# Cosine attention and a highway layer on one core: separate PSUM tiles for the gate and highway halves of the late output tiles, another split of work between engines, and another planned order

## The chip, the cores and the metric

The kernel runs on one core of a Trainium2 chip. The metric is the device time of one execution in microseconds (us). Most numbers here are medians of several executions; a profile is one execution, taken apart by the hardware profiler. An execution counts as slow when it is over 1.5% above the fastest of the same kernel, else as fast. Ratios use fast executions alone; a median is of all of them, and where some were slow the text says so.

In the profile's lines PE is TensorE, PEld its weight loads, DVE VectorE, ACT ScalarE, POOL GpSimd and SP SyncE. A row of a timeline gives start and duration in us, engine, line of the kernel, operation, the tile written and the tiles read, shapes and count; in brackets the idle time before it and what ended that.

## The reference

```python
# q, k, v: (8, 12, 448, 64) float32, tau = 0.1; w_h, w_t: (768, 768); b_t: (768,)
q_n = q / (norm(q) + 1e-6);  k_n = k / (norm(k) + 1e-6)
attn = softmax(q_n @ k_n.T / tau) @ v            # per batch and head
x = attn.transpose(0, 2, 1, 3).reshape(3584, 768)
H = relu(x @ w_h)
T = sigmoid(x @ w_t + b_t)
out = T * H + (1 - T) * x
```

## The kernel before

The work is cut in 24 head groups of four heads (an index Q) and 28 output tiles of 128 tokens (an index n), each of which is done in two halves of 384 columns. A head group's q and k are squared, summed and normalized, turned (transposed, by TensorE, or by a DMA transpose), multiplied to scores in PSUM (tile `sp`), put through exp (ACT), and multiplied with v (tile `u`); VectorE divides and writes x. An output tile turns x, multiplies it with the gate's weights and the highway's weights, and joins the two. T is computed with tanh, so that each half takes, on VectorE, a bias step (unless the bias is added by one more matmul), and two or three steps to join gate, highway and x.

The kernel doesn't issue instructions in the order of its loops. Each piece of work is recorded as an operation with an engine, a planned duration, its dependencies and a due time; then a planner on the host picks, for each engine, what comes next. Its choice weighs start against due time:

```python
    LAT = {"PE": 260, "ACT": 170, "DVE": 150, "POOL": 150, "SP": 0}
    LATE = 0.025
...
                    k = (max(s, t + self.NEAR) + (e != "SP") * self.LATE * 1000 * o.pri, o.pri, o.n)
...
            if o.size:                                   # a transfer: its share of the DMA engines
                dma_free = max(dma_free, end + 900) + o.size
                o.done = dma_free + 1100
```

Tables of letters say which engine does a piece, one letter per head group or output tile (D DVE, A ACT, P POOL; for XT, S is a DMA transpose; for GATE, R is the three-step form and D and P compute a gate product on that engine; for BIAS, M adds the bias by matmul; for VM, U casts a group's v in two halves on DVE):

```python
    XT = "DDDDDDSDSAASSSSSSDSSSSSSDAAA"
    GATE = "RRRRRRRRRRRRRRRRRRRRPPPPRRRR"
    BIAS = "MMMMMMMMMMMMMMMMMMMMMMDDDDDD"
    VM = "AAAAAAUDUDDDDDDDUDDDAAAA"
    TAIL = 6
```

The last six output tiles (`tail`) come after all scores, so they may use the score tiles. Gate (w_i = 1) and highway (w_i = 0) of a half share one tile of two banks:

```python
            tail = n >= 28 - TAIL
            if not tail:
                ringq, waitq = P.buf("pt", 2)
            elif w_i == 1:
                ringq, waitq = P.buf("sp", 2)
...
                    if tail and w_i == 1 and grp[0] == 0:
                        loc["sp", mh] = s_ps.tile([128, 2, 512], FP32, name="sp")
                    if grp[0] == 0:
                        loc["pt", qi] = (
                            loc["sp", mh][:, 1 - w_i, 0:MH] if tail
                            else p_ps.tile([128, MH], FP32, name="pt", tag="pt")[:, :]
                        )
```

Of the kernel before, what the change touches and what calls it, by code (L numbers as in the profile page):

```python
# [8 lines left out]
FP32 = mybir.dt.float32  # L9
# [11 lines left out]
class Plan:  # L21
# [6 lines left out]
    SLACK = 1.3  # L28
    AHEAD = 15
    NEAR = 60  # L30
    LATE = 0.025

    def __init__(self):
        self.ops = []
# [20 lines left out]
    def run(self):  # L55
        for o in self.ops:
            deps, after = {}, {}
            for d in o.deps:
                if isinstance(d, Op):
                    deps[d.n] = d  # L60
                elif d[0] == "all":
                    deps.update((x.n, x) for x in d[1] if x is not o)
                else:
                    after.update((x.n, x) for x in d[1][:1] if x is not o)
            o.after = [x for n, x in after.items() if n not in deps]
            o.deps = list(deps.values())
        t_eng = {e: 0 for e in self.LAT}
        left = {o.n: len(o.deps) + len(o.after) for o in self.ops}
        outs = {o.n: [] for o in self.ops}
        for o in self.ops:  # L70
            for d in o.deps + o.after:
                outs[d.n].append(o)
        ready = {e: [] for e in self.LAT}
        users = {n: len(c) for n, c in outs.items()}
        back = [o for o in self.ops if not users[o.n]]
        while back:
            o = back.pop()
            due = 1e9 if o.pri is None else o.pri[0] if isinstance(o.pri, tuple) else o.pri
            for c in outs[o.n] if not isinstance(o.pri, tuple) else ():
                lat = o.dur + self.LAT[o.eng] + (o.size + 2000 if o.size else 0)  # L80
                due = min(due, c.pri - (self.SLACK * lat / 1000 if o in c.deps else 0))
            o.pri = due
            for d in o.deps + o.after:
                users[d.n] -= 1
                if not users[d.n]:
                    back.append(d)

        def arm(o):
            r = 0
            for d in o.deps:  # L90
                r = max(r, d.done + (100 if d.eng == o.eng else self.LAT[d.eng]))
            for d in o.after:
                r = max(r, d.start)
            if o.eng == "SP":
                r += 300
            if o.kind == "load":
                r = max(r, 1000 * (o.pri - self.AHEAD))
            if o.kind == "at":
                r = max(r, 1000 * o.pri)
            ready[o.eng].append((r, o))  # L100

        for o in self.ops:
            if not left[o.n]:
                arm(o)
        order = []
        mode = ""
        port = [0, 0]
        dma_free = 0
        lanes = []
        while len(order) < len(self.ops):  # L110
            best = None
            for e, L in ready.items():
                if not L:
                    continue
                t = t_eng[e]
                pick = None
                for r, o in L:
                    s = max(t, r)
                    if e == "DVE" and o.kind == "lock":
                        s = max(s, port[0])  # L120
                    elif e == "POOL":
                        s = max(s, port[1])
                    elif e == "SP" and len(lanes) >= 8:
                        s = max(s, lanes[-8])
                    if e == "SP":
                        s = max(s, dma_free - 5000)
                    k = (max(s, t + self.NEAR) + (e != "SP") * self.LATE * 1000 * o.pri, o.pri, o.n)
                    if pick is None or k < pick[0]:
                        pick = (k, s, r, o)
                if best is None or pick[1] < best[1]:  # L130
                    best = pick
            _, s, r, o = best
            e = o.eng
            ready[e].remove((r, o))
            end = s + o.dur
            if e == "PE":
                if o.kind != mode:
                    end += self.SWITCH
                mode = o.kind
            elif e == "POOL":  # L140
                port[0] = end
            elif e == "DVE" and o.kind == "lock":
                port[1] = end
            t_eng[e] = end
            o.start, o.done = s, end
            if o.size:
                dma_free = max(dma_free, end + 900) + o.size
                o.done = dma_free + 1100
            if e == "SP":
                lanes.append(o.done)  # L150
            order.append(o)
            for c in outs[o.n]:
                left[c.n] -= 1
                if not left[c.n]:
                    arm(c)
        return order
# [6 lines left out]
def kernel(  # L163
# [13 lines left out]
    B, NH, S, D = q.shape  # L177
# [40 lines left out]
    ones_row = const.tile([128, 128], FP16)  # L218
    eps = const.tile([128, 1], FP32)
    NV = 2  # L220
    SQ_E = ("DPAAAAAAPAAAAAPAADPAAAAP", "PPAPPPPPPAAPAAAAAAPPPPPP")
    FOLDS = "000000000002012110000110"
    NORM = ("DDDPPDPPPPPPPPPPPPPPDPPP", "DPPPPPPPPPPPPPPPPPPPPDPP")
    TURN = ("ADDDSSSSSSSSSSSSSSSSSSSS", "DDDDASSSSSSSSSSSSSSSSSSS")
    XT = "DDDDDDSDSAASSSSSSDSSSSSSDAAA"
    ENG = {"A": "ACT", "D": "DVE", "P": "POOL"}
    PAIR = 12
    GATE = "RRRRRRRRRRRRRRRRRRRRPPPPRRRR"
    BIAS = "MMMMMMMMMMMMMMMMMMMMMMDDDDDD"
    LATER = 3  # L230
    W_AT = 16
    RS = "AAAAAAADDDDDDDDDDDDDDDDD"
    SW_AT = 48
    VM = "AAAAAAUDUDDDDDDDUDDDAAAA"
    TAIL = 6
    vm_b = [const.tile([128, 6, C, 66], FP16, name=f"vm{i}") for i in range(NV)]
    e_b = [const.tile([128, 14 * S + 64], FP16, name=f"e{i}") for i in range(2)]
# [40 lines left out]
    def load_qk(Q):  # L278
# [4 lines left out]
        for t in range(2):  # L283
            def f(t=t):
                if t == 0:
                    st["raw", Q] = raw_p.tile([128, NG, D], FP32, name="raw")
                eng = nc.scalar if Q == 0 and t else nc.sync
                eng.dma_start(
                    st["raw", Q][:, NT * t : NT * t + NT].rearrange("x (h c) d -> x h (c d)", h=2),
                    (q, k)[t][b, 4 * qd : 4 * qd + 4]  # L290
                    .rearrange("n (p c) d -> (n p) (c d)", c=C)
                    .rearrange("(h x) f -> x h f", x=128),
                )
            o = op("SP", 60 if Q == 0 and t else 550, None, wait, f, kind="load", size=1300)
            wait = [("first", [o])] + wait if not got else wait
            got.append(o)
            ring.append(o)
        st["got", Q] = got

    def load_v(b):  # L300
# [4 lines left out]
        for i in range(NQ):  # L305
# [7 lines left out]
                    .rearrange("(i x) f -> x i f", x=128),  # L313
                )

            o = op("SP", 550, None, [("first", ring[:1])] + wait if i else wait, f, kind="load", size=1300)
            ring.append(o)
            st["gotv", b].append(o)

# [191 lines left out]
    def norms(Q, rs_op):  # L511
        b, qd = divmod(Q, NQ)
        for t in range(2):
# [50 lines left out]
            else:  # L564
# [4 lines left out]
                        st["qn", Q, t][:, :, :].rearrange("p c x -> p (c x)"),  # L569
                    )  # L570

                z = op("SP", 1230, None, done + wait2, g, size=1330)
                ring += [z]
            ring2.append(z)
            st["turned", Q, t] = z
# [180 lines left out]
    def ffn(b, t, F, n):  # L756
# [25 lines left out]
            nc.sync.dma_start_transpose(loc["xT"][:, :, :], xf())  # L782

        if XT[n] == "S":
            c = a = op("SP", 1100, None, need + waitt, td, size=1140)
        else:
            ringp, waitp = P.buf("pt", 2)
            a = op("PE", 300, None, need + waitp, tr, kind="full")
# [6 lines left out]
    def quarters(b, t, F, n, loc, c, ringt, ring_x, xf, later):  # L795
        ringo, waito = P.buf("o", N_O)
        fin = []
        for qi, (w_i, mh) in enumerate(((1, 0), (0, 0), (1, 1), (0, 1))):
# [1 line left out]
            if qi == LATER:  # L800
                later()
            tail = n >= 28 - TAIL
            if not tail:
                ringq, waitq = P.buf("pt", 2)
            elif w_i == 1:
                ringq, waitq = P.buf("sp", 2)
            when = F + 1.6 * qi
            by_mm = BIAS[n] == "M"
            groups = ((0, 1, 2), (3, 4, 5, 6)) if w_i == 1 and by_mm else ((0, 1, 2), (3, 4, 5))
            mms = []  # L810
            for gi, grp in enumerate(groups):
                def mm(grp=grp, w_i=w_i, ms=ms, mh=mh, qi=qi, tail=tail, by_mm=by_mm):
                    if tail and w_i == 1 and grp[0] == 0:
                        loc["sp", mh] = s_ps.tile([128, 2, 512], FP32, name="sp")
                    if grp[0] == 0:
                        loc["pt", qi] = (
                            loc["sp", mh][:, 1 - w_i, 0:MH] if tail
                            else p_ps.tile([128, MH], FP32, name="pt", tag="pt")[:, :]
                        )
                    for cc in grp:  # L820
# [5 lines left out]
                        )  # L826
                m = op("PE", 163 * len(grp), when + 0.5 * gi,
                       [c, w_done[w_i][gi]] + w_done[2:] * (len(grp) == 4)
                       + ([("first", mms[:1])] if mms else [("first", mms_t[:1])] if tail and w_i == 0 else waitq),
                       mm, kind="full")  # L830
                mms.append(m)
            ringq += mms
            ringt += mms

            if w_i == 1:
                mms_t = mms
                ready = mms[-1]
                if not by_mm:
                    def fb(qi=qi, ms=ms):
# [119 lines left out]
    for Q in range(NQUAD):  # L959
# [6 lines left out]
        elif qd == NQ - 1:  # L966
            o = rsqrt(b, 0, NQ, reds[Q - 2] + reds[Q - 1] + reds[Q])
            for i in range(NQ):
                rs_of[Q - i] = o

    for Q in range(NQUAD):
        norms(Q, rs_of[Q])
    for b in range(B):
        cast_v(b)
        for qd in range(NQ):
            quad(NQ * b + qd)
    todo = []
    for b in range(B):
        f0 = slot_t[NQ * (b + 1)] + 5
        for t in [0, 1, 2] + ([3] if b % 2 else []):  # L980
            todo.append((b, t, f0 + 6.3 * t, len(todo)))
    nxt = [ffn(*todo[0])]

    def more(i):
        if i < len(todo):
            nxt.append(ffn(*todo[i]))

    for i in range(len(todo)):
        nxt[i](lambda i=i: more(i + 1))

    for o in P.run():
        o.fn()
# [35 lines left out]
```

## Time and profile before

| | before |
|---|---|
| time, median of 3 runs | 288.83 us (287.86 to 289.18) |
| span in the profile | 286.2 us |
| last exp ends | 239.8 us |
| last matmul ends | 279.6 us |
| last VectorE step ends | 282.0 us |
| the output lands | 4.2 us later |

The page's first part gives busy time, share of the span and instruction count of each engine:

```profile
PE 241.4 (84%) x4223; PEld 135.9 (47%) x4223; DVE 225.7 (79%) x481; ACT 206.5 (72%) x283; POOL 155.6 (54%) x166
```

No engine stands above 84%, because this is an average over stages that have different limits. One term is needed for the rest of this document: **the tail** is the time from the end of the last exp to the end of the last VectorE step. It is 42.1 us here.

### The profile page before, as it was taken

What the parts mean: (1) busy time and instruction counts of PE and PEld (TensorE: products, weight loads), DVE (VectorE), ACT (ScalarE), POOL (GpSimd) and SP (SyncE); (2) the same over time, 40 slices, a digit from 0 to 9 for tenths busy, and PEclk for the clock granted to TensorE, in tenths of its full rate; (3) what the DMA queues carried; (4) which work ended last, traced back from release to release, by engine and by line L of the source; (5) the groups of instructions that cost most, each with busy time, mean ns of one, the idle gap of its engine ahead of it and who ended that gap; (6) DMA issues with size and microseconds to landing.
All of it is one profiled execution on the core that took longest, in us unless ns stands there. A gap on an engine that the chain in (4) does not pass through costs nothing.

```text
span 286.2 us, 9911 instructions
## 1 busy us (share of the span) xinstructions
PE 241.4 (84%) x4223; PEld 135.9 (47%) x4223; DVE 225.7 (79%) x481; ACT 206.5 (72%) x283; POOL 155.6 (54%) x166
## 2 busy tenths in 40 slices
PE   0278869998998999989989999989999998877660
PEld 0235544554455456454555555555555545544330
DVE  3878876799999979898999999999557454666662
ACT  1599999998985899976987978767897775112210
POOL 3878878536549964993595859708500253620000
PEclk9999999999999999999999999999999999999996
DMA  7999979999999999999999999967954342111112
GB/s 260 382 383 293 210 179 272 243 372 227 351 259 196 250 319 280 217 304 257 264 194 276 247 326 250 240 115 117 170 127 120 85 66 76 55 57 55 57 55 55
DMA packets 72860, 59.14 MB, mean 207 GB/s; under 512 B 49136, under 2 KB 69104, under 8 KB 72816
## 3 DMA queue, kind: packets, MB, share of 16 engines
q1 hardware_dynamic: 70944, 55.69, 76.3%
q0 software_dynamic: 1600, 2.36, 4.6%
q8 instruction: 33, 0.54, 0.8%
q10 hardware_dynamic: 272, 0.46, 0.4%
q14 instruction: 11, 0.09, 0.2%
HBM read 38.14 MB, written 11.01 MB: 172 GB/s over the span
## 4 chain that ended last, share of the span: by engine, by line
PE 38%; DVE 31%; ACT 13%; POOL 7%; issue 5%; DMA 3%; ACTq 0%; DVEq 0%; POOLq 0%
PE pt L821 17%; ACT e L634 8%; PE u L674 8%; PE sp L623 7%; PE sp L821 5%; DVE o L915 4%; DVE n L391 4%; DVE pt L893 3%; DVE pt L908 3%; POOL qn L527 3%; DVE x L725 3%; ACT tt L850 2%; DVE sp L840 2%; DVE vm L586 2%; DVE qn L527 2%
## 5 line engine op out<-in xcount | busy, mean ns | idle before, releaser
L634 ACT ACTIVATE e<-sp 128x896 f16<-128x896 f32 x168 | 145.8, 928 | 25.2 <-PE sp L623 24.4
L527 POOL TENSOR_TENSOR qn<-raw,rs 128x448 f16<-128x448 f32 x82 | 81.1, 1021 | 41.6 <-DVE rs L493 34.4
L821 PE MATMUL pt<-w,xT 128*128 128x384 f16 x528 | 102.4, 327 | 1.2 <-ACT tt L850 0.6
L821 PEld LDWEIGHTS <-xT 128*128 128x128 f16 x672 | 58.9, 98 | 61.1 <-issue 26.6
L674 PE MATMUL u<-vm,e 64*128 64x65 f16 x2688 | 57.6, 191 | 6.6 <-DVE x L725 4.5
L674 PEld LDWEIGHTS <-e 64*128 64x128 f16 x2688 | 47.3, 95 | 30.9 <-issue 18.2
L623 PE MATMUL sp<-qT,qT 64*64 64x448 f16 x672 | 55.3, 373 | 5.9 <-ACT e L634 4.5
L391 DVE TENSOR_REDUCE n<-sq 128x7 f32<-128x448 f16 x68 | 39.3, 610 | 1.1 <-ACT sq L367 0.3
L821 PE MATMUL sp<-w,xT 128*128 128x384 f16 x144 | 26.2, 325 | 10.0 <-DVE sp L840 8.9
L893 DVE SCALAR_TENSOR_TENSOR pt<-tt,pt 128x384 f32<-128x384 f16 x44 | 24.7, 562 | 7.7 <-PE pt L821 4.6
L623 PEld LDWEIGHTS <-qT 64*64 64x64 f16 x672 | 15.7, 105 | 29.0 <-issue 23.8
L371 POOL TENSOR_TENSOR sq<-raw 128x448 f16<-128x448 f32 x20 | 20.1, 1007 | 16.4 <-DMA raw<-in_k_dram 7.9
L908 DVE SCALAR_TENSOR_TENSOR pt<-pt,x 128x384 f32<-128x384 f32 x36 | 20.2, 561 | 8.6 <-PE pt L821 8.3
L850 ACT ACTIVATE tt<-sp 128x384 f16<-128x384 f32 x12 | 5.9, 491 | 29.0 <-PE sp L821 25.9
L850 ACT ACTIVATE tt<-pt 128x384 f16<-128x384 f32 x44 | 21.7, 493 | 6.7 <-PE pt L821 3.4
L367 ACT ACTIVATE sq<-raw 128x896 f16<-128x896 f32 x26 | 24.4, 967 | 1.6 <-POOL fold L418 0.7
L725 DVE TENSOR_TENSOR x<-u,rd 128x384 f16<-128x384 f32 x48 | 24.6, 551 | 0.7
L915 DVE SCALAR_TENSOR_TENSOR o<-x,pt 128x384 f32<-128x384 f16 x36 | 19.9, 552 | 1.0
L375 POOL TENSOR_TENSOR sq<-raw 128x448 f16<-128x448 f32 x20 | 20.1, 1007 | 0.0
L707 DVE RECIPROCAL rd<-u 128x12 f32<-128x12 f32 (+1 forms) x48 | 9.7, 202 | 10.0 <-PE u L674 9.4
L418 POOL TENSOR_TENSOR fold<-sq 128x448 f32<-128x448 f16 x14 | 14.8, 1064 | 4.7 <-ACT sq L367 4.6
L551 PE MATMUL tp<-ident,qn 128*128 128x128 f16 x63 | 6.4, 260 | 12.0 <-DVE qn L527 11.5
(56 smaller groups left out, 180.0 us busy)
## 6 DMA issues: line engine op xcount, KB each, us to landing
raw<-in_q_dram SPq DMA_DIRECT2D x24, 448.0 KB, 6.1
vr<-in_v_dram SPq DMA_DIRECT2D x24, 448.0 KB, 6.1
raw<-in_k_dram SPq DMA_DIRECT2D x23, 448.0 KB, 6.0
out_dram<-o SPq DMA_DIRECT2D x24, 384.0 KB, 3.3
out_dram<-o SPq DMA_DIRECT2D x8, 192.0 KB, 3.2
w<-in_moe_w_t_dram POOLq DMA_DIRECT2D x2, 576.0 KB, 9.7
w<-in_moe_w_h_dram POOLq DMA_DIRECT2D x2, 576.0 KB, 11.5
qT<-qn SPq DMA_TRANSPOSE x39, 4.6
```

Source lines behind the costliest of these rows:

```text
L367: nc.scalar.activation(o, i, AF.Square)
L391: nc.vector.reduce_sum(n2[:, qd, NT * t + g0 : NT * t + g0 + n], src()[:, g0 : g0 + n, 0:width], axis=AX.X,)
L527: (nc.vector if eng == "DVE" else nc.gpsimd).tensor_mul(st["qn", Q, t][:, :, :].rearrange("p c (h d) -> p h c d", h=2)[:, h0:h1, c0:c1, :] ...
L623: nc.tensor.matmul(sp[64 * half : 64 * half + 64, h, 0:S].rearrange("x (c p) -> x c p", c=C), lhsT=kT[hp, ci, 64 * half : 64 * half + 64], ...
L634: nc.scalar.activation(e[:, o : o + 2 * S].rearrange("x (a p c) -> x a p c", a=2, c=C), st["sp", Q, ci][:, :, 0:S].rearrange("x a (c p) -> ...
L674: nc.tensor.matmul(u[:, s, slot * (D + 1) : (slot + 1) * (D + 1)], lhsT=e[sp, o : o + 128], rhs=vm[sp, 2 * qd + h, c, 0 : D + 1], start=(c ...
L725: nc.vector.tensor_mul(st["x", b][:, :, 4 * qd : 4 * qd + 4, :].rearrange("p t (h s) d -> p t h s d", s=2)[:, :, :, s, :], u[:, s, :, 0:D] ...
L821: nc.tensor.matmul(loc["pt", qi], lhsT=loc["xT"][:, cc, :] if cc < CC else ones_row[:, :], rhs=w_f[w_i][:, cc, ms] if cc < CC else bth[:, ms],
L850: nc.scalar.activation(loc["tt", mh][:, :], loc["pt", qi], AF.Tanh)
L893: nc.vector.scalar_tensor_tensor(out=h, in0=loc["tt", mh][:, :], scalar=1.0, in1=h, op0=ALU.add, op1=ALU.mult)
L908: nc.vector.scalar_tensor_tensor(out=h, in0=h, scalar=0.0, in1=xf()[:, ms], op0=ALU.max, op1=ALU.subtract)
L915: nc.vector.scalar_tensor_tensor(out=loc["o"][:, ms], in0=xf()[:, ms], scalar=2.0, in1=loc["pt", qi], op0=ALU.mult, op1=ALU.add,)
```

## The change

Its intent: late tiles get their gate in a score tile and their highway in one of the one-bank tiles; x is turned by TensorE in tiles 0 to 13 and 16, by DMA in the others; squares, folds, casts, gates and biases are shared out anew; and the planner gets other weights, costs for DMA transposes, and an interleaved declaration of head groups and output tiles.

```diff
-    LATE = 0.025
+    LATE = 0.04
...
-                r = max(r, d.done + (100 if d.eng == o.eng else self.LAT[d.eng]))
+                r = max(r, d.done + (120 if d.eng == o.eng else self.LAT[d.eng]))
...
-                dma_free = max(dma_free, end + 900) + o.size
+                dma_free = max(dma_free, end + (-700 if o.kind == "turn" else 900)) + o.size
...
-    SQ_E = ("DPAAAAAAPAAAAAPAADPAAAAP", "PPAPPPPPPAAPAAAAAAPPPPPP")
-    FOLDS = "000000000002012110000110"
-    NORM = ("DDDPPDPPPPPPPPPPPPPPDPPP", "DPPPPPPPPPPPPPPPPPPPPDPP")
+    SQ_E = ("APAAAAAAPAAAAAPAPAPAAAAP", "PPAPPPPPAAAAAAAAAAPPPAAA")
+    FOLDS = "000000010102012120000110"
+    NORM = ("DDDPPPPPPPPPPPPPPPPPDPPP", "DPPPPPPPPPPPPPPPPPPPPDPP")
-    XT = "DDDDDDSDSAASSSSSSDSSSSSSDAAA"
+    XT = "DDDDDDDDAAAAADSSASSSSSSSSSSS"
-    GATE = "RRRRRRRRRRRRRRRRRRRRPPPPRRRR"
-    BIAS = "MMMMMMMMMMMMMMMMMMMMMMDDDDDD"
+    LEAD = 4
+    GATE = "RRRRRRRRRDRRRRRPRRDRPPPRPRRD"
+    BIAS = "MMMMMMMMMMMMMMMDDDMMDDDDDDDM"
-    VM = "AAAAAAUDUDDDDDDDUDDDAAAA"
+    VM = "UAAUAAUUDUUDDUDDUDDUUUUU"
...
-                z = op("SP", 1230, None, done + wait2, g, size=1330)
+                z = op("SP", 1230, None, done + wait2, g, kind="turn", size=1950)
...
-            if not tail:
-                ringq, waitq = P.buf("pt", 2)
-            elif w_i == 1:
-                ringq, waitq = P.buf("sp", 2)
+            in_s = tail and w_i == 1
+            ringq, waitq = P.buf("sp" if in_s else "pt", 2)
...
-                    if tail and w_i == 1 and grp[0] == 0:
-                        loc["sp", mh] = s_ps.tile([128, 2, 512], FP32, name="sp")
...
-                            loc["sp", mh][:, 1 - w_i, 0:MH] if tail
+                            s_ps.tile([128, 2, 512], FP32, name="sp")[:, 0, 0:MH] if in_s
...
+    for Q in range(NQUAD):
+        norms(Q, rs_of[Q])
+        if Q % NQ == 0:
+            cast_v(Q // NQ)
+        quad(Q)
+        while made < len(todo) and (Q == NQUAD - 1 or made * 6 <= (Q - LEAD) * 7):
...
```

(Cut: planned sizes of other transfers, one due time, the planner's own wait of a late highway for its gate, and the loops that the last one replaces.)

More of the change, by code (lines that the diff above doesn't have):

```diff
@@ L232 @@
     RS = "AAAAAAADDDDDDDDDDDDDDDDD"
-    SW_AT = 48
-    VM = "AAAAAAUDUDDDDDDDUDDDAAAA"
+    SW_AT = 52
+    VM = "UAAUAAUUDUUDDUDDUDDUUUUU"
     TAIL = 6
@@ L293, in f @@
                 )
-            o = op("SP", 60 if Q == 0 and t else 550, None, wait, f, kind="load", size=1300)
+            o = op("SP", 60 if Q == 0 and t else 550, None, wait, f, kind="load", size=1200)
             wait = [("first", [o])] + wait if not got else wait
@@ L314, in f @@
                 )
-            o = op("SP", 550, None, [("first", ring[:1])] + wait if i else wait, f, kind="load", size=1300)
+            o = op("SP", 550, None, [("first", ring[:1])] + wait if i else wait, f, kind="load", size=1200)
             ring.append(o)
@@ L784, in ffn @@
         if XT[n] == "S":
-            c = a = op("SP", 1100, None, need + waitt, td, size=1140)
+            c = a = op("SP", 1100, None, need + waitt, td, kind="turn", size=1670)
         else:
@@ L811, in quarters, with mm @@
             for gi, grp in enumerate(groups):
-                def mm(grp=grp, w_i=w_i, ms=ms, mh=mh, qi=qi, tail=tail, by_mm=by_mm):
-                    if tail and w_i == 1 and grp[0] == 0:
-                        loc["sp", mh] = s_ps.tile([128, 2, 512], FP32, name="sp")
+                def mm(grp=grp, w_i=w_i, ms=ms, mh=mh, qi=qi, in_s=in_s, by_mm=by_mm):
                     if grp[0] == 0:
                         loc["pt", qi] = (
-                            loc["sp", mh][:, 1 - w_i, 0:MH] if tail
+                            s_ps.tile([128, 2, 512], FP32, name="sp")[:, 0, 0:MH] if in_s
                             else p_ps.tile([128, MH], FP32, name="pt", tag="pt")[:, :]
@@ L828, in quarters @@
                        [c, w_done[w_i][gi]] + w_done[2:] * (len(grp) == 4)
-                       + ([("first", mms[:1])] if mms else [("first", mms_t[:1])] if tail and w_i == 0 else waitq),
+                       + ([("first", mms[:1])] if mms else waitq),
                        mm, kind="full")
@@ L835, in quarters @@
             if w_i == 1:
-                mms_t = mms
                 ready = mms[-1]
@@ L969 @@
                 rs_of[Q - i] = o
-    for Q in range(NQUAD):
-        norms(Q, rs_of[Q])
-    for b in range(B):
-        cast_v(b)
-        for qd in range(NQ):
-            quad(NQ * b + qd)
     todo = []
@@ L981 @@
             todo.append((b, t, f0 + 6.3 * t, len(todo)))
-    nxt = [ffn(*todo[0])]
+    nxt = []
     def more(i):
@@ L986, in more @@
             nxt.append(ffn(*todo[i]))
-    for i in range(len(todo)):
-        nxt[i](lambda i=i: more(i + 1))
+    made = 0
+    for Q in range(NQUAD):
[4 more added lines that the diff above has]
+        while made < len(todo) and (Q == NQUAD - 1 or made * 6 <= (Q - LEAD) * 7):
+            if not made:
+                more(0)
+            i = made
+            made += 1
+            nxt[i](lambda: more(i + 1))
     for o in P.run():
```

## The prediction

> **What bounds the kernel now.** I began with the busy row by slices, to see whether one limit holds over the whole span (286.2 us in the trace, 288.83 us timed, so the timed number lies 2.6 us above the span).
>
> ```profile
> PE   0278869998998999989989999989999998877660
> ...
> DVE  3878876799999979898999999999557454666662
> ACT  1599999998985899976987978767897775112210
> ...
> DMA  7999979999999999999999999967954342111112
> ```
>
> A slice is 7.2 us. There are three stages. Up to slice 27 (about 195 us) PE and DVE are both at nine tenths, and the DMA engines too. From 195 to 240 us PE alone is full. From 240 us on nobody is full: PE falls to 6 to 8 tenths, DVE to 5 or 6, and ACT and DMA are nearly idle. A table of stretches (start:end and length, then busy us and count of PE, PEld, DVE, ACT, POOL, then clock, DMA share, GB/s) puts numbers to it:
>
> ```profile
> 165.00:180.00 15.00, 14.73 (x234) 7.47 (x232) 14.14 (x33) 10.97 (x16) 11.56 (x13) 1.00 1.02 267
> ...
> 210.00:225.00 15.00, 14.84 (x250) 8.05 (x252) 8.82 (x19) 12.77 (x18) 0.00 (x0) 1.00 0.36 84
> 239.00:254.00 15.00, 12.23 (x202) 7.62 (x200) 9.97 (x21) 2.81 (x6) 7.30 (x8) 1.00 0.14 55
> 254.00:282.00 28.00, 17.79 (x108) 9.87 (x108) 17.87 (x35) 6.10 (x11) 0.00 (x0) 0.99 0.15 57
> ```
>
> The last two rows are the tail: the last exp ends at 239.8 us, and six of the 28 output tiles (numbers 22 to 27) are still to do. PE is idle for 2.8 + 10.2 = 13.0 us there. Who keeps whom waiting, after 240 us:
>
> ```profile
> ACT tt L850 <- PE sp L821: 25.9, 10, 3.6
> ...
> PE sp L821 <- DVE sp L840: 8.9, 10, 1.4
> DVE sp L908 <- ACT tt L850: 8.5, 8, 1.3
> ```
>
> The timeline of one half tile shows the loop that these waits form:
>
> ```profile
> 262.46 0.56 DVE L840 SCALAR_TENSOR_TENSOR sp<-b_all,sp 128x384 f32<-128x384 f32 x1
> 263.07 2.11 PE L821 MATMUL sp<-w,xT 128*128 128x384 f16 x12 [1.09 <-DVE sp L840]
> ...
> 263.80 0.49 ACT L850 ACTIVATE tt<-sp 128x384 f16<-128x384 f32 x1 [2.36 <-PE sp L821]
> 264.33 0.57 DVE L908 SCALAR_TENSOR_TENSOR sp<-sp,x 128x384 f32<-128x384 f32 x1 [1.31 <-ACT tt L850]
> 264.93 0.56 DVE L893 SCALAR_TENSOR_TENSOR sp<-tt,sp 128x384 f32<-128x384 f16 x1
> 265.40 0.56 DVE L840 SCALAR_TENSOR_TENSOR sp<-b_all,sp 128x384 f32<-128x384 f32 x1
> ```
>
> The gate's bias (L840, DVE) ends, only then the highway matmuls start; the tanh of the gate (L850) starts only after the first three of them, though it reads none of their output; and the highway's first DVE step (L908) starts only after the tanh, though it reads none of that. All three are false waits: gate and highway are two halves of one PSUM tile, and dependencies are kept for the whole tile. The biases of alternate halves fall at 255.98, 262.46, 268.93 and 275.41: 6.47 us a tile, with some 4.2 us of matmuls in it (24, 12 of which took 2.11).
>
> **What the Trainium skill says.** "PSUM — Partial Sum Buffer", section "PSUM bank collisions raise a hardware error": collisions are by bank and quadrant, and two engines on different banks run clean. The two halves lie 512 fp32 apart, a bank each, so the waits above protect nothing; the trace shows them all the same (8.9 us for PE). "Perfetto Trace Analysis", section "Matmuls": independent groups should rotate through different banks, so that an evacuation overlaps the next matmuls. The tail has the banks and doesn't get the overlap. The same page, "Identifying the Most-Contended Engine", judges TensorE by weight loads rather than matmul busy time: PEld is 8.05/15 = 0.54 at 210 to 225 us, 7.47/15 = 0.50 at 165 to 180 and 9.87/28 = 0.35 in the tail. So the tail has real room, the middle little. "DMA: Bandwidth & Descriptors", section "DMA Transpose (X-bar)": such transposes take 2-byte data and write to SBUF. x is f16, and the trace has 14 x transposes by DMA, 2.7 to 6.4 us to landing, median 3.5.
>
> **The change, part by part.**
>
> *Separate tiles in the tail.* Gates of tiles 22 to 27 keep one score buffer each; highways go to the other ring of two one-bank buffers, which stood unused but for transposes. All three false waits go. What remains per half is 12 matmuls = 2.11 us of PE, or the DVE steps at about 0.60 us from start to start (264.33 to 264.93). New settings: tiles 22 and 24 have the gate product on POOL (3 DVE steps a half), 23, 25 and 26 have 4, and 27 has 3 (bias by matmul again). DVE: 2 x 0.60 x (3+4+3+4+4+3) = 25.2 us, plus the last two head groups' reciprocals and products, 2 x (0.23+1.02+0.19+0.43) = 3.7, together 28.9. PE: 6 x 4.2 = 25.3, plus 182 attention matmuls still to come after 238 us, about 3.5: 28.8. The two are equal, so neither will be full: I take 10 to 15% idle, 32 to 33 us from 240 us on, in place of 42. Then the last output, as now: from the end of the last DVE step (281.96) to the span's end is 4.2 us. The tail gives 8 to 9 us.
>
> *Turning x.* Tiles 6, 8, 11, 12, 13 and 16 go from DMA to TensorE; 17 and 24 to 27 the other way. In the middle PE gains 5 x 0.50 = 2.5 us, and the full DMA engines lose five transposes of 192 KB net. In the tail PE loses 4 x 0.5 = 2 us and ACT and DVE their copies (0.79 and 0.56). The price is latency, 3.5 us against about 1.5 by matmul and copy. x of the last batch could be complete some 5 us after the last scores, while tiles 22 and 23 still hold 8.4 us of matmuls, so I count it hidden.
>
> *Bias.* Eighteen tiles in place of 22 add it by matmul: 8 fewer at 0.165 us (13 took 2.22, 10 took 1.73), PE -1.3 us. DVE +4 tiles x 2 x 0.56 = +4.5 us, of which tiles 15 to 17 (3.4 us) fall in the full stage.
>
> *Other DVE work.* Two squares leave (2 x 1.458 = -2.9); folds on POOL at three more places shorten sums (4 x 0.61 + 2 x 0.23 = -2.9); one normalization leaves (-1.3); one more gate on POOL (-1.1). Casts of v: from 11 whole and 6 halves (14.1 us) to 7 and 26: 7 x 0.985 + 26 x 0.61 = 22.8, +8.7. The sum with the bias is +5.0, but casts of groups 20 to 23 (4.9) and biases of tiles 20 and 21 (2.2) fall at 195 to 240 us where DVE is 59% busy or less, and those of groups 0 and 3 (2.4) before 60 us. In the full stage DVE loses some 2 us net. ACT: 6 more squares (+5.8), 6 fewer casts (-5.7), one more copy: even. POOL: +5.8 folds, +2.0 normalization, -8.1 squares, +3.6 gates = +3.3 of 155.6; it stays far from a bound.
>
> *The order.* Head groups and output tiles are now declared interleaved, but who takes which PSUM buffer in turn stays the same: tiles 22 on are still declared after the last head group. What changes is the pick: a weight of 0.04 in place of 0.025 on how early a piece is due, and higher planned costs of transposes by DMA. I can't work out its effect from the profile; in the middle, with PE +1.5 and DVE -2 us, I put it at 0, give or take 3 us.
>
> **The rivals.** First: the tail turns DVE-bound, with 4-step tiles at 4.8 us. For it: DVE's 28.9 us equals PE's and the DVE steps can't overlap. Against: 6.47 us a tile is far above 4.8 anyway. It would leave a gain of 6 to 7 us, about 282. Second: the transposes by DMA become the wait that replaces the false ones, if the attention of the last group is done late, as now (x at 252.5 us). Then tiles 24 to 27 start 2 to 4 us later: about 283. Third: the middle slows, since PE and DVE both stand at 94% and more and PE gets five more turns; +3 us, also about 283. Fourth: the middle gains, since DMA was full (share 1.02 at 165 to 180) and the chain shows a wait of 5.1 us for a q or k transpose at 177 us; fewer x transposes could give 3 to 5 us: about 275.
>
> **Range and chances.** 288.8 - 8.5 (tail) - 0.8 (PE's own sum over the kernel, -1.3 + 0.5) = 279.5 us. Failing overlap in the tail and a slower middle together reach 285; a gain in both stages reaches 273. Faster by 2% means below 283.1: one rival alone doesn't prevent it, two do, so 0.78; within 2%: 0.19; slower: 0.03.
>
> **What would show it.** After the last exp no wait of the tanh for highway matmuls, and none of those for L840's bias; tiles 25 and 26 at 4.2 to 5 us; PE idle of 4 to 6 us in place of 13 before the last matmul. The last exp at 237 to 242 us, if the middle is even. The prediction is wrong if the last exp moves by more than 4 us, if a wait for a transposed x of over 2 us opens in the tail, or if DVE stays under 75% busy there without PE being full.

## The result, and the profile after

The changed kernel takes 274.05 us (median of 4 runs, 272.78 to 275.56), the kernel before 289.0 us (4 runs). The ratio is 0.948, with a 95% interval of 0.941 to 0.956. Ratios here are the mean time of one kernel's fast runs over that of the other's fast runs of the same rounds, so they aren't quite the ratio of the medians. The time lies inside the predicted range, 1 us above its lower end; the gain of 15.0 us is larger than the 9.3 us forecast.

The slices of the profile after (span 273.3 us, so a slice is 6.8 us):

```profile
PE   0277769989799999999999999999899999998991
DVE  2998767599789989888999999899998787578793
```

In the tail PE now stays at eight or nine tenths up to the last slice but one, where before it fell to between eight and six from slice 33 on. The same from the table of stretches (columns as in the prediction), from the last scores to the last matmul:

```profile
238.50:254.00 15.50, 14.74 (x217) 9.28 (x214) 12.64 (x28) 4.12 (x7) 5.68 (x7) 1.00 0.40 112
254.00:267.50 13.50, 13.24 (x81) 7.64 (x79) 11.85 (x25) 3.43 (x7) 3.35 (x4) 1.00 0.31 103
```

PE is idle for 0.76 + 0.26 = 1.0 us of 29.0. The waits after 240 us (who for whom: us, times, longest):

```profile
ACT tt L846 <- DVE sp L836: 19.2, 10, 3.2
POOL g L857 <- ACT tt L846: 9.5, 2, 7.5
ACT tt L846 <- PE sp L818: 1.9, 2, 1.6
DVE o L896 <- POOL g L861: 1.5, 3, 0.9
DVE pt L889 <- ACT tt L846: 1.2, 2, 0.6
PEld L818 <- DMA xT<-x: 0.9, 1, 0.9
```

The two big rows are idle time of ACT and POOL, which no longer bound anything: the tanh (L846) waits for its own bias step (L836), as it must. Of the false waits there is no trace: no matmul waits for a bias, and where the tanh waits for matmuls (1.9 us), it is in tile 27, whose gate gets its bias by matmul. A half tile in the timeline of the changed kernel:

```profile
261.04 0.56 DVE L836 SCALAR_TENSOR_TENSOR sp<-b_all,sp 128x384 f32<-128x384 f32 x1
261.16 1.14 PE L818 MATMUL sp<-w,xT 128*128 128x384 f16 x6
...
261.69 0.49 ACT L846 ACTIVATE tt<-sp 128x384 f16<-128x384 f32 x1 [1.69 <-DVE sp L836]
...
262.14 1.14 PE L818 MATMUL pt<-w,xT 128*128 128x384 f16 x6
...
263.11 0.56 DVE L836 SCALAR_TENSOR_TENSOR sp<-b_all,sp 128x384 f32<-128x384 f32 x1
```

From bias to bias it is 2.07 us, where before a whole tile took 6.47, so 3.24 a half. PE goes from gate to highway to the next gate without a gap, beside the bias and the tanh. And the stages as a whole:

| | before | after |
|---|---|---|
| last exp ends | 239.8 us | 240.2 us |
| tail (last exp to last VectorE step) | 42.1 us | 28.7 us |
| PE idle, last scores to last matmul | 10.6 us | 1.0 us |
| last VectorE step to the end of the span | 4.2 us | 4.4 us |

So in these two executions the whole gain, 13.4 us, lies in the tail. The questions are how much of it the separate tiles made, and by which mechanism, and what tables and order are good for if the middle is as long as before.

### The profile page after: what moved, and what is told of

The parts are those of the page before. It is cut to its first block, busy times and chain, and to the rows that moved or that the text cites. A ratio compares the mean times of both kernels' runs of the same rounds, so it can differ in the third digit from the quotient of the medians.

```text
span 273.3 us, 9928 instructions
## 1 busy us (share of the span) xinstructions
PE 240.0 (88%) x4221; PEld 135.8 (50%) x4221; DVE 226.7 (83%) x496; ACT 207.4 (76%) x284; POOL 154.7 (57%) x170
## 5 line engine op out<-in xcount | busy, mean ns | idle before, releaser
L818 PE MATMUL pt<-w,xT 128*128 128x384 f16 x600 | 117.2, 329 | 3.7 <-DVE o L911 1.6
L528 POOL TENSOR_TENSOR qn<-raw,rs 128x448 f16<-128x448 f32 x84 | 78.9, 970 | 42.2 <-DVE rs L494 37.5
L624 PE MATMUL sp<-qT,qT 64*64 64x448 f16 x672 | 56.2, 376 | 4.8 <-ACT e L635 3.4
L392 DVE TENSOR_REDUCE n<-sq 128x7 f32<-128x448 f16 x60 | 34.4, 609 | 5.6 <-ACT sq L368 5.6
L889 DVE SCALAR_TENSOR_TENSOR pt<-tt,pt 128x384 f32<-128x384 f16 x56 | 31.4, 560 | 8.7 <-ACT tt L846 4.9
L368 ACT ACTIVATE sq<-raw 128x896 f16<-128x896 f32 x32 | 30.2, 967 | 4.7 <-DMA raw<-in_q_dram 4.4
L624 PEld LDWEIGHTS <-qT 64*64 64x64 f16 x672 | 15.7, 105 | 29.1 <-issue 24.4
L846 ACT ACTIVATE tt<-pt 128x384 f16<-128x384 f32 x44 | 21.9, 498 | 9.3 <-DVE pt L836 5.4
L419 POOL TENSOR_TENSOR fold<-sq 128x448 f32<-128x448 f16 x18 | 18.7, 1058 | 9.1 <-ACT sq L368 9.1
L372 POOL TENSOR_TENSOR sq<-raw 128x448 f16<-128x448 f32 x16 | 16.1, 1009 | 13.0 <-DMA raw<-in_k_dram 7.0
L846 ACT ACTIVATE tt<-sp 128x384 f16<-128x384 f32 x12 | 5.9, 490 | 21.1 <-DVE sp L836 19.2
L587 DVE CAST vm<-vr 128x448 f16<-128x448 f32 (+1 forms) x33 | 21.5, 673 | 0.1
L857 POOL TENSOR_TENSOR g<-tt,x 128x384 f16<-128x384 f16 x8 | 7.3, 910 | 16.9 <-ACT tt L846 16.9
L376 POOL TENSOR_TENSOR sq<-raw 128x448 f16<-128x448 f32 x16 | 16.1, 1005 | 0.0
```

Of the source, the lines that this page charges most:

```text
L368: nc.scalar.activation(o, i, AF.Square)
L392: nc.vector.reduce_sum(n2[:, qd, NT * t + g0 : NT * t + g0 + n], src()[:, g0 : g0 + n, 0:width], axis=AX.X,)
L528: (nc.vector if eng == "DVE" else nc.gpsimd).tensor_mul(st["qn", Q, t][:, :, :].rearrange("p c (h d) -> p h c d", h=2)[:, h0:h1, c0:c1, :] ...
L624: nc.tensor.matmul(sp[64 * half : 64 * half + 64, h, 0:S].rearrange("x (c p) -> x c p", c=C), lhsT=kT[hp, ci, 64 * half : 64 * half + 64], ...
L818: nc.tensor.matmul(loc["pt", qi], lhsT=loc["xT"][:, cc, :] if cc < CC else ones_row[:, :], rhs=w_f[w_i][:, cc, ms] if cc < CC else bth[:, ms],
L846: nc.scalar.activation(loc["tt", mh][:, :], loc["pt", qi], AF.Tanh)
```

## The experiments

All kernels gave correct results. One caution holds for all of them: since a planner sets the order, an edit of one table moves instructions everywhere. The tail is therefore read from the trace of each run beside the time.

### The separate tiles alone

To the kernel before, only the tile code was applied:

```diff
-            if not tail:
-                ringq, waitq = P.buf("pt", 2)
-            elif w_i == 1:
-                ringq, waitq = P.buf("sp", 2)
+            in_s = tail and w_i == 1
+            ringq, waitq = P.buf("sp" if in_s else "pt", 2)
...
```

> The kernel before with nothing but the separate PSUM tiles in the tail (same settings, same planning weights). Theory (the false waits between the halves are the whole of the tail's idle time): PE idle between the last scores and the last matmul falls from 12.9 us to under 4 us, the last exp stays near 240 us, and the time is 277 to 281 us. Rival (the other order, which brings the attention of the last group forward, earned most): 284 us or more, with PE still idle for over 8 us.

Measured: 279.75 us, ratio 0.970 (0.966 to 0.974). The last exp ends at 240.4 us, the tail is 33.6 us, PE is idle for 4.0 us. The theory's numbers hold (the 12.9 us of its text count 2.4 us after the last matmul; before it, 10.6 us fell to 4.0), and 8.5 us of the tail went with the tiles alone. But the false waits weren't the whole of the idle time. Nearly all of the 4.0 us that are left are waits of TensorE for the turning of x:

```profile
PE pt L817 <- ACT xT L778: 2.7, 3, 0.9
PE xp L773 <- DVE x L725: 1.1, 1, 1.1
```

Some 5 us of the changed kernel's gain in the tail, then, come from something else.

### One tile again, all else new

> The changed kernel with gate and highway of late tiles back in one PSUM tile; settings and order stay new. Theory: some 10 us come back, 283 to 287 us, and the waits of the tanh for highway matmuls and of these for the bias are there again. Rival (order and settings earned most): under 279 us.

The edit is the reverse of the one above, on the changed kernel. Measured: 283.6 us (282.6 without one slow run of 286.65), ratio 0.981 (0.975 to 0.986). The tail is 38.2 us and PE is idle for 9.1 us. The waits of this run's tail:

```profile
ACT tt L851 <- PE sp L822: 21.7, 8, 4.3
...
PE sp L822 <- DVE sp L841: 5.2, 6, 1.6
DVE sp L909 <- ACT tt L851: 3.8, 5, 0.9
```

They are the three false waits of the kernel before, back in their places. From both sides the tiles are worth 8.5 to 9.5 us of tail (42.1 to 33.6; 38.2 to 28.7).

### The order alone, the tables alone

```diff
-    LATE = 0.025
+    LATE = 0.04
...
-    for b in range(B):
-        cast_v(b)
-        for qd in range(NQ):
-            quad(NQ * b + qd)
+    for Q in range(NQUAD):
+        norms(Q, rs_of[Q])
...
```

> The kernel before with the new planning weights and the interleaved declaration only. Theory: within 3 us of before, 286 to 292 us, because the tail keeps its false waits. Rival: 283 us or less.

Measured: 287.64 us, ratio 0.998 (0.993 to 1.004). The tail of its profile is 40.2 us, 2 us less than before, and its last exp ends at 243.7 us, 4 us later; the profile is of the slowest of its four runs. By itself the order is worth nothing that can be told from zero.

```diff
-    XT = "DDDDDDSDSAASSSSSSDSSSSSSDAAA"
-    GATE = "RRRRRRRRRRRRRRRRRRRRPPPPRRRR"
+    XT = "DDDDDDDDAAAAADSSASSSSSSSSSSS"
+    GATE = "RRRRRRRRRDRRRRRPRRDRPPPRPRRD"
...
```

> The kernel before with the new tables only (which engine squares, folds, casts, turns x, carries gate and bias). Theory: within 3 us of before, or slightly slower, since the tables were made for another plan; tiles 22 and 24 with the gate product on POOL and tile 27 with the bias by matmul shorten the loop of the tail by one DVE step each, which is worth up to 3 us. Rival (turning x by DMA frees PE in the tail and earned most): 283 us or less.

Measured: runs of 294.07, 289.0, 296.14 and 296.94 us, of which only the one of 289.0 counts as fast, so there is no ratio; the profiled run is slow. The rival's 283 us is out of reach. The tables alone are no gain, and probably a loss. (The text miscounts the tail's steps: tile 22 had its gate product on POOL before, and tile 23 loses it, so that the six tiles save one step a half, not three.)

### Tiles and tables without the order

```diff
-    LATE = 0.04
+    LATE = 0.025
...
-                z = op("SP", 1230, None, done + wait2, g, kind="turn", size=1950)
+                z = op("SP", 1230, None, done + wait2, g, size=1330)
...
```

> The changed kernel with the old planning weights and the old declaration order (so: before + separate tiles + new tables). The tables alone, on the old order, were no gain (289 us at best), the order alone 0.2%. Theory A (tables and order belong together: each was chosen for the other): 277 us or more. Theory B (order is worth nothing, the tables gain once the tail is split): 272 to 276 us.

Measured: 284.28 us, ratio 0.988 (0.984 to 0.992). Theory A's number holds: tables and order have to be judged together. The tail is 30.0 us, nearly that of the changed kernel, but the last exp ends at 248.6 us in place of 240.2. So the order, worth nothing alone, is worth 10 us once the tables are there, and the place where it earns that is the middle: without it the tables lose there more than they gain in the tail (279.75 us with the old tables, 284.28 with the new). The ends of the exps show where. After 36 of 168 exps this run is 5.2 us behind the changed kernel (64.3 to 59.1 us), after 66 level with it (103.2 to 103.3; the second profile of the changed kernel, of which more below, has 100.4), after 72 it is 7.1 us behind (117.7 to 110.6).

The trace of this run shows one thing that stands out, a v cast on VectorE:

```profile
100.24 5.42 DVE L586 CAST vm<-vr 128x896 f16<-128x896 f32 x1
```

In the changed kernel a whole cast takes 0.62 us in the two cases with no POOL work beside it, and 0.81 to 1.32 us beside POOL; half casts take 0.58 to 0.62 us either way. The run of the tables alone has the long cast too (5.43 us). Beside this one, POOL works without a gap up to 105.17 us:

```profile
98.33 3.62 POOL L527 TENSOR_TENSOR qn<-raw,rs 128x448 f16<-128x448 f32 x4
101.91 2.03 POOL L418 TENSOR_TENSOR fold<-sq 128x448 f32<-128x448 f16 x2
103.90 1.27 POOL L424 TENSOR_TENSOR fold<-fold 128x224 f32<-128x224 f32 x2
```

The Trainium skill, "SBUF — State Buffer", section "Who interferes with whom", says that a VectorE cast in a two-port mode and POOL lock each other out of a shared port pair. The trace agrees as far as it goes: the cast ends half a microsecond after POOL's last fold. TensorE was idle for 4.48 us up to 107.77 us, for VectorE's steps that stood in the queue behind the cast. I took it for the cause of the loss and tested that.

### The long cast taken away

```diff
-    VM = "UAAUAAUUDUUDDUDDUDDUUUUU"
+    VM = "UAAUAAUUUUUDDUDDUDDUUUUU"
```

> The kernel of the run order_back (new tables and separate tiles on the old order, 284.3 us) with one entry of the table of casts changed: the v cast of head group 8 in two halves in place of one whole. In order_back one whole cast on DVE took 5.42 us (100.24 to 105.66 us), where the others take 0.9 on average, while POOL ran without a gap. Theory (that one cast, locked out by POOL's work, is most of what the tables lose on the old order): no cast over 1.6 us, the last exp 4 to 6 us earlier (from 248.6 to 243 to 245 us), 278 to 281 us. Rival (the old order is slower for many small reasons and the cast's stall is hidden): 282.5 us or more.

Measured: 285.47 us (282.04 to 287.7; one slow run, without it 285.01), ratio 0.986 (0.981 to 0.991), against 0.988 with the long cast. The long cast is gone (the longest is 1.28 us), and the time doesn't fall: by the time the rival was right, and my theory fell. In the profile (of the fastest of the four runs) the six exps after the 66th take 9.3 us in place of 14.5, 7.3 in the changed kernel, but the 66th itself comes later (105.1 us), and the last exp ends at 245.9 us: 2.7 us earlier, where 4 to 6 were expected, and no more than executions of one program differ by (see the last experiment). What stands in the same place of the trace now is a wait of the scores. SyncE's queue, and ACT and PE:

```profile
98.94 5.14 SPq L567 DMA_TRANSPOSE qT<-qn  x2
```

```profile
101.73 0.95 ACT L367 ACTIVATE sq<-raw 128x896 f16<-128x896 f32 x1 [3.33 <-POOL fold L418]
102.59 2.51 ACT L634 ACTIVATE e<-sp 128x896 f16<-128x896 f32 x3
103.54 0.54 PE L623 MATMUL sp<-qT,qT 64*64 64x448 f16 x4 [2.86 <-ACT e L634]
```

The exp that released the scores is the first of the three in ACT's row; it ended at 103.48 us. It stood in ACT's queue behind a square, which had waited 3.33 us for a fold on POOL. So with the cast and without it, a queue stands behind POOL here. The two transposes of q and k, issued from 98.94 us on after three loads of 448 KB, are not the wait: the trace has them landed at 105.82 and 106.62 us, when the scores had gone on. Nor do slow landings tell the orders apart: a q or k transpose takes up to 9.8 us to land in this run and 6.2 in the changed kernel, but 9.9 in the run of the order alone. Which part of the new order (declaration, weights or planned sizes) saves the 10 us no run shows; the cause stays open.

### How x is turned

```diff
-    XT = "DDDDDDDDAAAAADSSASSSSSSSSSSS"
+    XT = "DDDDDDSDSAASSSSSSDSSSSSSDAAA"
```

> The changed kernel with the old choice of how x is turned (tiles 24 to 27 by TensorE, six tiles of the middle by DMA). Theory: in the tail TensorE gets 24 transposes, some 2 us, and they take buffers of the highway's ring, so the tail from the last exp to the last DVE step grows from 28.7 to 31 to 33 us; the time is 276 to 279 us. Rival (the turning is hidden either way): within 1 us of 274.

Measured: 281.75 us, ratio 0.978 (0.974 to 0.983), more than the 276 to 279 us expected. The tail is 32.9 us, as expected; the rest, some 3.5 us, would be the middle's. The one profile (last exp at 241.1 us) can't tell it from what executions of one program differ by (see the last experiment), but all four runs (280.05 to 283.27 us) lie above all ten of the changed kernel (271.64 to 276.27), so that five more DMA transposes in the middle may well cost something there; no run separates it. Two of the waits in its tail:

```profile
ACT xT L779 <- PE xp L774: 3.0, 3, 1.1
...
PE pt L818 <- ACT xT L779: 1.8, 2, 0.9
```

A turn by TensorE costs more than its six matmuls: ACT must copy the result out, and the transposed tile sits in a buffer of the ring that the highways now need (`pt`).

### Gate and bias tables

```diff
-    GATE = "RRRRRRRRRDRRRRRPRRDRPPPRPRRD"
-    BIAS = "MMMMMMMMMMMMMMMDDDMMDDDDDDDM"
+    GATE = "RRRRRRRRRRRRRRRRRRRRPPPPRRRR"
+    BIAS = "MMMMMMMMMMMMMMMMMMMMMMDDDDDD"
```

> The changed kernel with the old tables for gate product and bias (tiles 20 to 23 gate on POOL, 24 to 27 four DVE steps a half, 22 tiles with the bias by matmul). Theory: TensorE +8 matmuls = 1.3 us before the tail, DVE in the tail 2 x 0.6 x (3+3+4+4+4+4) = 26.4 in place of 25.2 us and one step more at the very end: 275 to 277 us, tail 30 to 31 us. Rival (DVE is what bounds the tail once it is split): tail over 32 us.

Measured: 277.82 us, ratio 0.964 (0.960 to 0.968); the tail is 32.8 us, the last exp ends at 237.0 us. The tail grew by 4.0 us, more than the 1 to 2 expected and as much as the rival said. The trace splits it in three: PE is idle for 2.5 us, 1.5 more than in the changed kernel, and 2.3 us of that is a wait for a DMA transpose of x; it has 1.0 us more to do after the last scores (220 products with v are left there, in place of 140); and 1.5 us more pass between the last matmul and the last VectorE step, where tile 27 now takes four steps a half. VectorE is busy for 23.2 of the 31.4 us from the last scores to the last matmul, so it doesn't bound the whole; in the last 15.7 us (254.0 to 269.7) it is busy for 14.4, and there the rival may be right.

### What in the separate tiles does it

The prediction spoke of false waits inside a half. But separate tiles do a second thing: the gate's buffer comes free after its tanh and not after the last step of its highway. To tell these apart, the next kernel keeps the separate tiles and reads one column of the gate's tile after the half's last step, so that the buffer stays taken:

```diff
+            def hold(gq=gate_qi):
+                nc.vector.tensor_copy(keep[:, :], loc["pt", gq][:, 0:1])
...
+                if tail:
+                    gate_q.append(op("DVE", 70, F + 6 + 3.2 * mh, [e2], hold))
```

> The changed kernel with one tiny DVE copy of one element per late half tile from the gate's PSUM tile after the half's last step (12 copies of about 0.1 us), so that the gate's buffer stays taken until its highway is finished, as it was when both shared a tile; the false waits inside a half stay away. Theory (the false waits inside a half are what the split removed): at most 3 us slower than the changed kernel, 274 to 277 us. Rival (the earlier release of the gate's buffer is what the split gave): 281 us or more.

Measured: 279.26 us, ratio 0.969 (0.963 to 0.974); the tail is 32.8 us. That is between the two theories. The copies took 0.15 us each, so a control was needed, with the same copies reading the output tile in SBUF:

```diff
-                nc.vector.tensor_copy(keep[:, :], loc["pt", gq][:, 0:1])
+                nc.vector.tensor_copy(keep[:, :], loc["o"][:, 0:1])
...
-                    gate_q.append(op("DVE", 70, F + 6 + 3.2 * mh, [e2], hold))
+                    ringo.append(op("DVE", 70, F + 6 + 3.2 * mh, [e2], hold))
...
```

> The control for the run gate_held (279.3 us): the same 12 tiny DVE copies at the same places, but reading the output tile in SBUF, so that no PSUM buffer stays taken. If the longer hold of the gate's buffer is what cost 5 us: 274 to 276 us. If the copies themselves cost it: 278 us or more.

Measured: 275.1 us, ratio 0.953 (0.950 to 0.956); the tail is 28.9 us, as in the changed kernel (28.7). So the copies cost nothing, and holding the gate's buffer costs 3.9 us of tail (32.8 - 28.9), about four tenths of the 9.5 us that the separate tiles are worth under the new tables. That is a difference of whole kernels: the planner knows of the hold and orders the tail anew. In the trace of the held kernel TensorE waits for a copy only 0.2 us; its longer waits are for the highways' own ring:

```profile
PE pt L819 <- DVE o L901: 1.5, 1, 1.5
PE pt L819 <- DVE o L916: 1.1, 1, 1.1
```

And the kernel with one tile again waits 5.2 of its 9.1 us for biases, but only 1.6 for the last step of an earlier half, which is the late release itself. So the hold does cost something, at most 3.9 us by these runs (some copies came up to 0.9 us after the half's last step); the rest, 5.6 us or more, is left for the false waits inside a half. How the two share the gain is by subtraction and not shown more closely.

### A try at a faster version, and the changed kernel again

```diff
-    XT = "DDDDDDDDAAAAADSSASSSSSSSSSSS"
-    BIAS = "MMMMMMMMMMMMMMMDDDMMDDDDDDDM"
+    XT = "DDDDDDADAAAADDSSSASSSSSSDSSS"
+    BIAS = "DMMMMMMMMMMMMMDDMDDMDDDDDDDM"
...
+                    eng = nc.scalar if b == B - 1 and i == 0 else nc.sync
```

> A try at a faster version: the changed kernel with tables varied once more (27 entries), and the last output's two halves issued from two queues. TensorE's bias matmuls move to DVE in three more places net; the last issue overlaps (-0.5 us). If the tail stays full: 271 to 274 us; if a cast or a wait of the middle goes wrong as in order_back: 276 us or more.

> The changed kernel once more, unchanged, beside the others on one chip: 273 to 276 us, ratio 0.945 to 0.955.

(The text miscounts its edit: 35 entries differ, and two more tiles have the bias on VectorE, net.) Measured: 277.13 us for the new try, or 276.5 without its slow run of 285.21, ratio 0.960 (0.957 to 0.963); the changed kernel again has 274.56 us (271.64 to 276.27), or 273.3 without two runs of 276.1 and 276.3 that count as slow, ratio 0.953 (0.950 to 0.957). The try is no better. Its profile fell in the slow state and isn't used.

The second profile of the changed kernel is worth more. Its tail is 28.75 us, within a hundredth of that in the first profile (28.74), but its last exp ends at 236.8 us in place of 240.2. The stretch from 70 to 80 us of the same program, first profile and second:

```profile
70.00:80.00 10.00, 7.67 (x72) 3.70 (x69) 7.08 (x19) 7.45 (x10) 6.85 (x8) 0.83 0.85 231
```

```profile
70.00:80.00 10.00, 8.99 (x107) 4.56 (x104) 9.73 (x25) 9.86 (x14) 6.85 (x8) 1.00 1.07 296
```

In the first PE, VectorE and ACT all did less, and the granted clock fell with it. What stalled there isn't known. So the middle varies by some 3 us between executions of one program: a difference of that size in the last exp proves nothing about a table, while the tail's length does (the two kernels of the old order have the same tail too, 29.97 us, with last exps 2.7 us apart).

## Why the prediction was right or wrong

| step of the prediction | predicted | measured |
|---|---|---|
| three false waits bound the tail | they go | gone; back in the run with one tile |
| what the tail gives | 8 to 9 us | 13.4 us; of it by the separate tiles 8.5 us alone, 9.5 us under the new tables |
| PE idle before the last matmul | 4 to 6 us, from 13 | 1.0 us, from 10.6 |
| tiles 25 and 26 | 4.2 to 5 us each | 4.43 us from tile 25's first bias (256.61) to tile 26's (261.04) |
| last exp | 237 to 242 us | 240.2 and 236.8 us |
| order | 0, give or take 3 us | 0 alone; 10 us once the tables are there |
| waiting for x turned by DMA | hidden | one wait of 0.8 us |
| time | 279.5 us (273 to 285) | 274.05 us |

**The bound was read rightly.** The stage, the loop, the three waits and the fact that the chip doesn't need them are all as the prediction had them, and so was the choice to look for the gain in the tail.

**The term that was mis-sized is the tail**, 8.5 us where 13.4 were measured. TensorE's work was summed rightly: 28.8 us from the last scores on (measured: 28.0). The step that failed is the 10 to 15% of idle time laid on top. Its reason was that VectorE's 28.9 us equal TensorE's, and that sum was too high: it took 0.60 us from one VectorE step to the next, from one pair of starts, while the next pair in the same lines is 0.47 us apart (264.93 to 265.40), so that steps do overlap. After the change four steps take 2.07 us, and VectorE is busy for 24.5 of 29.0 us. So there was no balance of two full engines, and TensorE was idle for 1.0 us in place of 4 to 6. Two smaller slips: the sum began at the last scores, 238 us, but its end was counted "from 240 us on", which alone is nearly 2 us; and the 13.0 us of idle time before the change count 2.4 us after the last matmul.

The separate tiles under the old tables do take 33.6 us with 4.0 us of idle time, so the guess fits that kernel, but by luck: there the idle time is waiting for x turned by TensorE (3.8 us), which the change removes. The 4.9 us between the two tails (33.6 and 28.7) are 2.9 us of idle time, 1.2 us of TensorE's work after the last scores, and 0.8 us between the last matmul and the last VectorE step. The prediction had counted the steps of the new tables in its sum, but had not given turning x and sharing out gate and bias a gain of their own in the tail. Undone one at a time, each costs about 4 us of tail there, although they can't both be added to the tiles' share (13.4 - 8.5 leaves 4.9).

**The mechanism was named, but not all of it.** The prediction said that gates "keep one score buffer each" and counted false waits only. That the buffer also comes free earlier is worth up to 3.9 us of the tail.

**The rivals.** VectorE doesn't bound the tail as a whole: it is busy for 84% of it, while PE is at 97%; in the tiles of four steps the two are close (256.61 to 263.11 us: VectorE busy for 6.0 of 6.5 us, PE for all). The DMA transposes were hidden but for 0.8 us. A slower or faster middle isn't shown. The fourth rival named 275 us, near what was measured, but the gain is in the tail: with the tail's length taken as fixed, the ten runs of the changed kernel (mean 274.2 us) put its last exp at 239.4 us, an estimate, 0.5 us before that of the profile before. TensorE's weight loads, by which the prediction judged its room, were busy for 0.58 of the tail after the change (16.9 of 29.0 us), above the 0.50 to 0.54 of the middle, so that these shares were no sign of a limit. And VectorE in the stretch from 195 to 210 us was busy for 76%, not for 59% or less.

**The order** was right in total and wrong in reason. The prediction could not work it out and put it at 0. It is large, but it is spent on making the new tables bearable: without it they end the last exp 8 us later. That the middle as a whole came out near 0 was luck.

## What to carry to other kernels

When two accumulations that different engines consume share one PSUM tile, look in the timeline for an engine that waits for work whose output it doesn't read, and give each its own tile: here that took 8.5 to 9.5 us from a tail of 42 us, by waits that vanish and, in part, by a buffer that comes free earlier. Estimate such a stage by summing each engine's work in it, with the cost of a step taken from several pairs and not from one, and let experiments and not habit say how much idle time lies on top. Where a planner orders the work, tables and order must be judged together, and a stage's own length in the trace tells more than the total when another stage varies by some us.

## What the Trainium skill lacked or had wrong

- "PSUM — Partial Sum Buffer", section "PSUM bank collisions raise a hardware error", says what the chip needs (banks and quadrants), and the runs agree. It doesn't say that a program's waits may be wider than that: here halves in two banks of one tile waited for each other, and PE lost 8.9 us to the bias alone.
- "Perfetto Trace Analysis", section "Matmuls", asks for independent groups in different banks. That was fulfilled before, and TensorE was still idle for 10.6 us of the tail; the section doesn't say that waits of the program, kept by the tile, can undo it.
- "SBUF — State Buffer", section "Who interferes with whom", has the loser block for the whole of the other's instruction, and gives no time for a cast that loses several times. In the changed kernel whole casts took 0.62 us without POOL beside them and 0.81 to 1.32 with it; in the run without the new order one took 5.42 us, across several POOL instructions in a row. That it was locked out all that time fits the rule, but no run shows it.
- "DMA: Bandwidth & Descriptors", section "DMA Transpose (X-bar)", has no figure for the time to landing beside other transfers: in the changed kernel x (192 KB) took 2.7 to 4.1 us, median 2.9, and q and k 2.9 to 6.2, median 4.4, with up to 9.8 and 9.9 us in two other runs.
